# Key-value products that share a quartered stretch with attention products, output copies on ScalarE, subtractions on VectorE, loads a tile sooner

## The chip, the cores and the metric

The kernel runs on one core of one Trainium2 chip. The metric is the device time of one execution in microseconds (us). The profile's engine names are used: PE is TensorE, PEld its weight loads, DVE is VectorE, ACT is ScalarE, POOL is GpSimd, SP is SyncE, whose queue issues most DMAs. L310 is line 310 of the kernel before.

## The reference

Linear attention followed by a two-layer network with a leaky ReLU. B = 8 batches, H = 8 heads, S = 576 rows, D = 64.

```python
def _attn_ref(q, k, v):
    q_s = q - np.max(q, axis=-1, keepdims=True)
    q_s = np.exp(q_s)
    q_s = q_s / (np.sum(q_s, axis=-1, keepdims=True) + 1e-09)
    k_s = k - np.max(k, axis=2, keepdims=True)
    k_s = np.exp(k_s)
    k_s = k_s / (np.sum(k_s, axis=2, keepdims=True) + 1e-09)
    kv = np.einsum('bhsd,bhse->bhde', k_s, v)
    return np.einsum('bhsd,bhde->bhse', q_s, kv)

def _moe_ref(x, w_in, w_out):        # x: (4608, 512), w_in: (512, 2048), w_out: (2048, 512)
    h = x @ w_in
    g = np.maximum(0.01 * h, h)
    return g @ w_out
...
x = attn_out.transpose(0, 2, 1, 3).reshape(B * S, H * D)
```

Queries are normalised over the head dimension, keys over the sequence; both are needed before the small 64x64 products of a batch can be used. Almost all arithmetic is in the two layers: 4608 tokens through 512x2048 and 2048x512.

## The kernel before

**Tiling.** The 4608 tokens are cut into nine tiles t = 0 to 8 of 512 tokens. Batches have 576 tokens, so the boundaries of batches and tiles drift against each other: tile t needs the attention output of batch t - 1 or t, up to all of batch t - 1 and the first part of batch t. Layer 1 of a tile is 16 output blocks j with 4 matmuls each (L488, 128x512, weights `w_in_sb`, moving `xT`) into a PSUM tile `ph`, which ScalarE turns into `gj` with the leaky function (L497). Layer 2 is four groups `tsub` of 16 matmuls each (L509) into `pout`, which is copied to `out_sb` by `store` (L503) and written out by two DMAs on SP's queue (L506). The copy is by ScalarE for the first two groups of tile 1 and by VectorE for the rest.

**The attention part of a batch b** runs in small pieces between these matmuls:

- `load_all(b)`: three loads (k, q, v, 1152 KB each, L80), issued on SP's queue, into a pool `raw` of six buffers, so two batches' worth.
- Keys: `k_tree` (maximum over nine rows, L150) and `k_allmax` (over partitions, L155 to L175) on VectorE, `k_sub` (L183, subtract the maximum; on GpSimd for batches 3 to 7), `k_exp` on ScalarE (L191) into `ke`.
- Values: `v_cast` (L203) to bf16 on GpSimd, into one of two buffers `vb`.
- Queries: `q_max` (L214, VectorE), `q_sub` (L273, GpSimd for batches 3 to 7), `q_exp` (L281, ScalarE) into `qe`, `q_sum` (L290, L292) and `q_norm` (L297) on VectorE, and `q_turn` (L481), a DMA transpose on SP's queue into `qX`.
- `kv(b)` (L310): 72 matmuls on quarters of the array (64x64, 65 columns), four side by side, into two PSUM tiles `pkv`; then `kd_make(b)` on VectorE (L329, L330) divides by the key sums into `kd`.
- `attend_all(b, ...)` (`cross`, L429): 16 quartered matmuls with `kd` as weights and `qX` moving, eight of 512 columns (rows 0 to 7) and eight of 64 (row 8), into six PSUM tiles `po`; `x_keep` (L452) copies them into `xT` on ScalarE, four copies of 512 columns and two of 128.

**What sets the order.** The schedule is written by hand. `at(t, u, fn)` puts a piece into slot u of tile t, and `run(t, u)` emits it: slots 0 to 15 come after each block j of layer 1, slots 16 to 31 after every fourth matmul of layer 2 (slot 16 + 4 x tsub + j // 4; the output copy of a group is emitted just ahead of its last slot). A slot number of 32 or more goes on into the next tile. Each engine works through its own queue in the order of emission and waits on semaphores for its operands; a slot fixes the order within an engine, not a time. Within one slot, pieces come in the order in which they were registered.

**Slots that matter here**, for batches 3 to 7 (`plan`, L643): with t = b - 2 and an offset o of 27 (batch 3), 22 (batch 4) or 17, the tree stands at slot o of tile t, all-max and key subtraction at o + 3, query maximum and subtraction at o + 7, key exponential at o + 11, casts at o + 12, query exponential at o + 16, sum at o + 18, normalise at o + 21, transpose at o + 22, `kv` at o + 24 or o + 25. So `kv` of batch 3 falls into slot 19 of tile 2, of batch 4 into slot 15 of tile 3, of batches 5 to 7 into slot 10 of tiles 4 to 6. `attend_all` stands at slot 27 of tile b - 1 for batches 3 and 4 and at slot 23 for 5 to 7. `load_all(b)` is at slot 2 of tile b - 2. Batch 2 has a plan of its own (`plan2`, L660); the second part of its attention products stands in slot 19 of tile 2, just ahead of `kv(3)`.

**PSUM.** `psB` has six one-bank buffers, used in turn by `ph`, `po`, `pkv` and the transposes of early batches; `psO` has two for `pout`.

Of the kernel before, what the change touches and what calls it, by code (L numbers as in the profile page):

```python
# [19 lines left out]
L = 64  # L20
# [5 lines left out]
def kernel(  # L26
# [104 lines left out]
    def k_begin(b):  # L131
        st[b]["ke"] = ke_pool.tile([P, R, HL, D], BF16, name="ke")
        st[b]["kmax"] = mx_pool.tile([P, HL, D], FP32, name="kmax")
        st[b]["kmaxT"] = mx_pool.tile([P, HL * D], FP32, name="kmaxT")
        st[b]["kall"] = mx_pool.tile([P, HL, D], FP32, name="kall")

    def k_tree(b, hs, steps=slice(0, 4)):
        n = hs.stop - hs.start
        ks = st[b]["k"][:, hs]
        if steps.start == 0:  # L140
            st[b]["t4"] = mx_pool.tile([P, HL, 4, D], FP32, name="t4")[:, 0:n]
        t4 = st[b]["t4"]
        t2, t1 = t4[:, :, 0:2], t4[:, :, 0]
        for o, i0, i1 in (
            (t4, ks[:, :, 0:4], ks[:, :, 4:8]),
            (t2, t2, t4[:, :, 2:4]),
            (t1, t1, t4[:, :, 1]),
            (st[b]["kmax"][:, hs], t1, ks[:, :, 8]),
        )[steps]:
            nc.vector.tensor_tensor(out=o, in0=i0, in1=i1, op=ALU.max)  # L150

    def k_allmax(b):


        nc.vector.transpose(  # L155
            out=st[b]["kmaxT"], in_=st[b]["kmax"].rearrange("p h d -> p (h d)")
        )
        m2 = small_pool.tile([P, CB, 2], FP32, name="m2")
        nc.vector.tensor_reduce(
            out=m2[:, :, 0],  # L160
            in_=st[b]["kmaxT"].rearrange("p (c j) -> p c j", j=32),
            axis=AX.X,
            op=ALU.max,
        )
        for a in range(4):
            o = a ^ 1
            nc.vector.tensor_reduce(
                out=m2[32 * o : 32 * o + 32, :, 1],
                in_=m2[32 * a : 32 * a + 32, :, 0:1],
                axis=AX.X,  # L170
                op=ALU.max,
            )
        m = small_pool.tile([P, CB], FP32, name="m")
        nc.vector.tensor_reduce(out=m, in_=m2, axis=AX.X, op=ALU.max)
        nc.vector.transpose(  # L175
            out=st[b]["kall"].rearrange("p h d -> p (h d)"),
            in_=m.unsqueeze(2).to_broadcast([P, CB, 32]),
        )

    def k_sub(eng, b, hs):  # L180
        ks = st[b]["k"][:, hs]
        n = hs.stop - hs.start
        eng.tensor_tensor(  # L183
            out=ks,
            in0=ks,
            in1=st[b]["kall"][:, hs].unsqueeze(2).to_broadcast([P, n, R, D]),
            op=ALU.subtract,
        )

    def k_exp(b, hs):  # L190
        nc.scalar.activation(  # L191
            out=st[b]["ke"][:, :, hs].rearrange("p r h d -> p h r d"),
            in_=st[b]["k"][:, hs],
            func=AF.Exp,
        )
# [10 lines left out]
    def q_begin(b):  # L206
        st[b]["qe"] = qe_pool.tile([P, R, HL, D], BF16, name="qe")
        if b < 2:
            st[b]["qT"] = qT_pool.tile([P, NB, R, L], BF16, name="qT", tag="qT")

    def q_max(b, rs, hs=ALLH):
        n, m = rs.stop - rs.start, hs.stop - hs.start
        st[b]["qmax", rs.start, hs.start] = o = small_pool.tile([P, HL, n], FP32, name="qmax")[:, 0:m]
        nc.vector.tensor_reduce(out=o, in_=st[b]["q"][:, hs, rs], axis=AX.X, op=ALU.max)  # L214
# [55 lines left out]
    def q_sub(eng, b, rs, hs=ALLH):  # L270
        n, m = rs.stop - rs.start, hs.stop - hs.start
        qs = st[b]["q"][:, hs, rs]
        eng.tensor_tensor(  # L273
            out=qs,
            in0=qs,
            in1=st[b]["qmax", rs.start, hs.start].unsqueeze(3).to_broadcast([P, m, n, D]),
            op=ALU.subtract,
        )

    def q_exp(b, rs, hs=ALLH):  # L280
        nc.scalar.activation(  # L281
            out=st[b]["qe"][:, rs, hs].rearrange("p r h d -> p h r d"),
            in_=st[b]["q"][:, hs, rs],
            func=AF.Exp,
        )
# [160 lines left out]
    def x_keep(eng, b, ggs, rows, hp):  # L446
# [6 lines left out]
        else:  # L453
            eng.tensor_copy(out=o, in_=ps)

    def attend_rows(b, rows, engs=(nc.scalar, nc.scalar)):
        groups = ((0, 1),) if rows.stop - rows.start <= 4 else ((0,), (1,))
        for ggs in groups:
            attend(b, ggs, rows)
        return [  # L460
            lambda ggs=ggs, hp=hp: x_keep(engs[hp], b, ggs, rows, hp) for ggs in groups for hp in range(2)
        ]
# [57 lines left out]
    def at(t, u, *fns):  # L520
        while t > 0 and u >= 32:
            t, u = t + 1, u - 32
        hooks.setdefault((t, u), []).extend(fns)
# [7 lines left out]
    def load_all(b):  # L531
        whole = [(ALLH, ALLR)]
        st[b]["k"] = load(k, b, "k_raw", whole)
        st[b]["q"] = load(q, b, "q_raw", whole)
        st[b]["v"] = load(v, b, "v_raw", whole)
# [101 lines left out]
    at(1, 25, lambda: q_transpose(1, 7, 2), lambda: q_keep(nc.scalar, 1, 7, 2))  # L637

    XR = (slice(0, 6), slice(6, R))
    for b in range(3, B):  # L640
        at(b - 2, 2, lambda b=b: load_all(b))

    def plan(b, o):  # L643
        t = b - 2
        at(t, o, lambda: k_begin(b), lambda: q_begin(b), lambda: k_tree(b, ALLH))
        at(t, o + 3, lambda: k_allmax(b), lambda: k_sub(nc.gpsimd, b, ALLH))
        at(t, o + 7, lambda: q_max(b, ALLR), lambda: q_sub(nc.gpsimd, b, ALLR))
        at(t, o + 11, lambda: k_exp(b, ALLH))
        at(t, o + 12, lambda: v_cast(nc.gpsimd, b, 0), lambda: v_cast(nc.gpsimd, b, 1))
        at(t, o + 16, lambda: q_exp(b, ALLR))  # L650
        at(t, o + 18, lambda: q_sum(b, ALLR))
        at(t, o + 21, lambda: q_norm(b, ALLR))
        kvu = o + (24 if b == 3 else 25)
        at(t, kvu, lambda: kv(b))
        at(t, kvu + 1, lambda: kd_make(b))
        at(t, o + 22, lambda: q_turn(b))
        at(b - 1, 27 if b < 5 else 23, lambda: attend_all(b, (slice(0, 8),), (slice(8, R),)))


    def plan2():  # L660
        b = 2
        at(1, 0, lambda: k_tree(b, H1))
        at(1, 3, lambda: k_allmax(b))
        at(1, 6, lambda: k_sub(nc.vector, b, H0), lambda: k_sub(nc.vector, b, H1))
        at(1, 9, lambda: k_exp(b, ALLH))
        for rs in XR:
            at(1, 9, lambda rs=rs: q_max(b, rs), lambda rs=rs: q_sub(nc.gpsimd, b, rs))
        at(1, 13, lambda: v_cast(nc.gpsimd, b, 0), lambda: v_cast(nc.gpsimd, b, 1))
        for i, rs in enumerate(XR):
            at(1, (14, 16)[i], lambda rs=rs: q_exp(b, rs), lambda rs=rs: q_sum(b, rs), lambda rs=rs: q_norm(b, rs))  # L670
            at(1, (15, 17)[i], lambda rs=rs: q_turn(b, rs))
        at(1, 23, lambda: kv(b))
        at(1, 24, lambda: kd_make(b))
        at(1, 27, lambda: attend_all(b, (XR[0],)), lambda: attend_all(1, (RE,)))
        at(2, 19, lambda: attend_all(b, (XR[1],)))

    plan2()
    for b in range(3, B):
        plan(b, {3: 27, 4: 22}.get(b, 17))


    def g_tiles():
# [69 lines left out]
    for t in range(1, NT):  # L752
        g_sb = []
        for j in range(NF):
            ph = psB_pool.tile([P, TT], FP32, name="ph", tag=BANK_TAG)
            layer1(j, ph, t * TT, TT)
            if j % 2 == 0:
                g_sb.append(g_pool.tile([P, 2, TT], BF16, name="gj"))
            leaky(g_sb[j // 2][:, j % 2], ph)
            run(t, j)  # L760
        for tsub in range(NTS):
            row0 = t * TT + tsub * P
            if row0 == T - P:
                for os, copy in ((slice(0, 384), nc.scalar.copy), (slice(384, O), nc.vector.tensor_copy)):
                    po = psB_pool.tile([P, os.stop - os.start], FP32, name="pout2", tag=BANK_TAG)
                    for j in range(NF):
                        layer2(po, g_sb, tsub, j, os)
                    store(row0, po, copy, os, (nc.sync, nc.scalar))
                break
            po = psO_pool.tile([P, O], FP32, name="pout", tag="pout")  # L770
            for j in range(NF):
                layer2(po, g_sb, tsub, j)
                if j == NF - 1:
                    store(row0, po, nc.scalar.copy if t == 1 and tsub < 2 else nc.vector.tensor_copy)
                if j % 4 == 3:
                    run(t, 16 + 4 * tsub + j // 4)
    assert not hooks, list(hooks)
# [30 lines left out]
```

## Time and profile before

| What | Value |
|---|---|
| Median of 3 runs | 284.26 us (284.12 to 284.36) |
| The profiled execution | 284.65 us |
| Its span, first to last instruction | 282.9 us |
| Granted TensorE clock, mean | 0.999 |
| ScalarE, `gj` (L497), 128x512, x144 | 602 ns each |
| ScalarE, `ke` (L191), 128x2304 | 2133 ns each |
| ScalarE, `qe` (L281), 128x2304 | 2131 ns each |
| VectorE, `out_sb` copy (L503), 128x512, x33 | 687 ns each |
| VectorE, `qmax` (L214), 128x2304 | 2539 ns each |
| VectorE, `qsum` (L290) and normalise (L297), 128x2304 | 2553 and 2558 ns each |
| GpSimd, key subtraction (L183), 128x2304, x5 | 5070 ns each |
| GpSimd, query subtraction (L273), 128x2304, x5 | 4056 ns each |
| GpSimd, value cast (L203), 128x1152, x14 | 1170 ns each |
| k, q, v loads of 1152 KB, median from issue to landing | 5.9, 8.2, 10.9 us |
| `qX` transposes, issue to landing, shortest, median, longest | 3.3, 4.8, 7.0 us |

The span is counted from the first to the last instruction of the program; the profiled execution's time has some 1.75 us more around it. A matmul record's length is not its share of the engine, since matmuls overlap: the distance from one start to the next is what counts. Tiles 2 to 6 last 29.2 to 29.4 us each (layer 1 of tile 2 begins at 77.7 us, of tile 3 at 107.1, of 4 at 136.3, of 5 at 165.5, of 6 at 194.6), tiles 7 and 8 27.6 us.

### The profile page before, as it was taken

To read this page: it belongs to the slowest core of one execution; us is meant where nothing else is said; L and a number is where in the kernel's file an instruction comes from. 1 tells how busy PE (TensorE), PEld (TensorE's weight loads), DVE (VectorE), ACT (ScalarE), POOL (GpSimd) and SP (SyncE) were. 2 spreads that over 40 slices of the span, in tenths; PEclk is the share of its full clock that TensorE was granted. 3 is DMA by queue.
4 is the path that set the end of the run, shared out by engine and by line. 5 is a ranking of instruction groups with operands and counts; after the bars stand their busy time and mean duration, and the time that the engine had idled before them with its cause. 6 is when DMAs were issued, how large, how long until landed. Compare 5 with 4: busy or idle time off the path is not lost.

```text
span 282.9 us, 4998 instructions
## 1 busy us (share of the span) xinstructions
PE 275.6 (97%) x2022; PEld 133.1 (47%) x2022; DVE 143.2 (51%) x241; ACT 146.2 (52%) x258; POOL 89.6 (32%) x62
## 2 busy tenths in 40 slices
PE   8799999999999999999999999999999999999994
PEld 3367654444444544444444444444444444444443
DVE  2974889989661992596293719371801100110021
ACT  3986564693369236912963377436843165026400
POOL 2846391053078029308700780069000000000000
PEclk9999999999999999999999999999999999999999
DMA  7999999994849166953597349733053200330033
GB/s 238 333 209 326 292 173 374 318 379 162 149 126 407 41 144 151 401 99 82 132 411 107 74 92 398 170 76 74 0 86 72 59 19 0 70 81 1 0 76 74
DMA packets 37175, 45.81 MB, mean 162 GB/s; under 512 B 16032, under 2 KB 20384, under 8 KB 37152
## 3 DMA queue, kind: packets, MB, share of 16 engines
q1 hardware_dynamic: 33680, 41.16, 49.4%
q0 software_dynamic: 3312, 4.20, 8.5%
q8 instruction: 16, 0.26, 0.4%
q10 hardware_dynamic: 160, 0.13, 0.1%
q14 instruction: 7, 0.06, 0.1%
HBM read 36.70 MB, written 9.44 MB: 163 GB/s over the span
## 4 chain that ended last, share of the span: by engine, by line
PE 90%; DMA 6%; POOL 2%; SPq 0%; issue 0%; DVE 0%
PE pout L509 44%; PE ph L488 42%; DMA w_in_sb<-in_moe_w_in_dram 3%; DMA k_raw<-in_k_dram 2%; PE pkv L310 2%; PE po L429 2%; POOL w_in_sb L123 1%; POOL vb L203 0%; PE psum_q L253 0%; SPq L80 0%; POOL qe L242 0%; PE psum_qt L402 0%; DVE out_sb L503 0%; POOL gate L559 0%; POOL gate L545 0%
## 5 line engine op out<-in xcount | busy, mean ns | idle before, releaser
L509 PE MATMUL pout<-w_out_sb,gj 128*128 128x512 bf16 (+2 forms) x592 | 127.9, 373 | 0.0
L488 PE MATMUL ph<-xT,w_in_sb 128*128 128x512 bf16 (+1 forms) x640 | 127.3, 358 | 0.2 <-DMA w_in_sb<-in_moe_w_in_dram 0.2
L497 ACT ACTIVATE gj<-ph 128x512 bf16<-128x512 f32 x144 | 81.8, 602 | 53.8 <-PE ph L488 53.4
L488 PEld LDWEIGHTS <-w_in_sb 128*128 128x128 bf16 x640 | 62.0, 98 | 62.1 <-DMA w_in_sb<-in_moe_w_in_dram 0.9
L509 PEld LDWEIGHTS <-gj 128*128 128x128 bf16 x592 | 56.4, 98 | 64.7 <-issue 0.2
L503 DVE COPY out_sb<-pout 128x512 f32<-128x512 f32 (+1 forms) x34 | 22.7, 675 | 89.9 <-PE pout L509 87.1
L183 POOL TENSOR_TENSOR k_raw<-k_raw,kall 128x2304 f32<-128x2304 f32 (+1 forms) x6 | 29.1, 4857 | 75.6 <-DVE kall L175 62.1
L452 ACT CAST xT<-po 128x512 bf16<-128x512 f32 (+3 forms) x43 | 17.0, 488 | 43.4 <-PE po L429 43.4
L273 POOL TENSOR_TENSOR q_raw<-q_raw,qmax 128x2304 f32<-128x2304 f32 (+4 forms) x12 | 32.3, 2694 | 22.1 <-DVE qmax L214 21.4
L290 DVE TENSOR_REDUCE qsum<-qe 128x36 f32<-128x2304 bf16 (+5 forms) x13 | 20.1, 1543 | 30.7 <-ACT qe L281 30.7
L297 DVE TENSOR_TENSOR qe<-qe,qrec 128x2304 bf16<-128x2304 bf16 (+5 forms) x13 | 22.3, 1717 | 0.4
L191 ACT ACTIVATE ke<-k_raw 128x2304 bf16<-128x2304 f32 (+2 forms) x11 | 17.6, 1603 | 6.6 <-POOL k_raw L183 5.4
L214 DVE TENSOR_REDUCE qmax<-q_raw 128x36 f32<-128x2304 f32 (+5 forms) x13 | 19.9, 1537 | 0.8 <-DMA q_raw<-in_q_dram 0.8
L281 ACT ACTIVATE qe<-q_raw 128x2304 bf16<-128x2304 f32 (+5 forms) x13 | 17.2, 1325 | 2.9 <-POOL q_raw L273 2.9
L203 POOL CAST vb<-v_raw 128x1152 bf16<-128x1152 f32 x14 | 16.0, 1170 | 0.0
L150 DVE TENSOR_TENSOR t<-k_raw 128x512 f32<-128x512 f32 (+1 forms) x11 | 10.2, 927 | 2.7 <-DMA k_raw<-in_k_dram 2.7
L150 DVE TENSOR_TENSOR t<-t 128x256 f32<-128x256 f32 (+2 forms) x22 | 9.9, 449 | 0.7
L503 ACT COPY out_sb<-pout 128x512 f32<-128x512 f32 (+1 forms) x3 | 1.7, 550 | 15.7 <-PE pout L509 15.7
L341 PE MATMUL pout<-zero 128*128 128x512 bf16 x24 | 8.3, 488 | 1.3 <-POOL zero L98 1.3
L310 PEld LDWEIGHTS <-ke 64*64 64x64 bf16 x576 | 5.8, 106 | 3.3 <-ACT gj L497 1.7
L310 PE MATMUL pkv<-vb,ke 64*64 64x65 bf16 x576 | 6.9, 194 | 0.2
L228 ACT ACTIVATE qe<-q_raw,nmax 128x64 bf16<-128x64 f32 x16 | 5.3, 333 | 3.5 <-DVE nmax L223 3.5
(59 smaller groups left out, 90.2 us busy)
## 6 DMA issues: line engine op xcount, KB each, us to landing
out_dram<-out_sb SPq DMA_DIRECT2D x70, 128.0 KB, 2.4
v_raw<-in_v_dram SPq DMA_DIRECT2D x7, 1152.0 KB, 10.9
q_raw<-in_q_dram SPq DMA_DIRECT2D x6, 1152.0 KB, 8.2
k_raw<-in_k_dram SPq DMA_DIRECT2D x5, 1152.0 KB, 5.9
k_raw<-in_k_dram SPq DMA_DIRECT2D x6, 576.0 KB, 6.2
w_in_sb<-in_moe_w_in_dram POOLq DMA_DIRECT2D x8, 256.0 KB, 7.7
w_out_sb<-in_moe_w_out_dram POOLq DMA_DIRECT2D x6, 256.0 KB, 11.4
v_raw<-in_v_dram SPq DMA_DIRECT2D x2, 576.0 KB, 7.5
```

What stands on the lines that cost most here:

```text
L150: nc.vector.tensor_tensor(out=o, in0=i0, in1=i1, op=ALU.max)
L183: eng.tensor_tensor(out=ks, in0=ks, in1=st[b]["kall"][:, hs].unsqueeze(2).to_broadcast([P, n, R, D]), op=ALU.subtract,)
L191: nc.scalar.activation(out=st[b]["ke"][:, :, hs].rearrange("p r h d -> p h r d"), in_=st[b]["k"][:, hs], func=AF.Exp,)
L214: nc.vector.tensor_reduce(out=o, in_=st[b]["q"][:, hs, rs], axis=AX.X, op=ALU.max)
L273: eng.tensor_tensor(out=qs, in0=qs, in1=st[b]["qmax", rs.start, hs.start].unsqueeze(3).to_broadcast([P, m, n, D]), op=ALU.subtract,)
L290: nc.vector.reduce_sum(out=qsum, in_=st[b]["qe"][:, rs, hs], axis=AX.X)
L297: nc.vector.tensor_tensor(out=qes, in0=qes, in1=st[b]["qrec", rs.start, hs.start].unsqueeze(3).to_broadcast([P, n, m, D]), op=ALU.mult,)
L310: nc.tensor.matmul(outs[hh][hp * D : (hp + 1) * D, 0 : D + 1], lhsT=st[b]["ke"][rows, r, 2 * gg + hp], rhs=vb2[b % 2][rows, r, gg, hp, 0 : ...
L488: nc.tensor.matmul(ph, lhsT=w_in_sb[:, cb, j * P : (j + 1) * P], rhs=xT[:, cb, c0 : c0 + n], start=(cb == 0 and first), stop=(cb == NB - 1 ...
L497: nc.scalar.activation(out=o, in_=ph, func=AF.Prelu, alpha=LEAKY_SLOPE)
L503: copy(out=out_sb, in_=pout)
L509: nc.tensor.matmul(pout, lhsT=g_sb[j // 2][:, j % 2, tsub * P : (tsub + 1) * P], rhs=w_out_sb[:, j, os], start=(j == 0), stop=(j == NF - 1),)
```

## The change

- **A new function `attend_kv(b)`** takes the place of `attend_all(b)` for batches 3 to 6. It emits the attention products of batch b for rows 0 to 7 as before, then takes two PSUM tiles that each hold row 8's attention products (128 columns) and, behind them, the key-value sums of batch b + 1 (2 x 66 columns); it emits row 8's products into the first part and then the 72 key-value matmuls of batch b + 1 into the second. `kd_make(b + 1)` follows on VectorE, and the six `x_keep` copies on ScalarE. So the key-value products of batches 4 to 7 no longer have slots of their own. Batch 3's stay at slot 19 of tile 2, and batch 7's attention keeps `attend_all`.
- **Subtractions** of keys and queries of batches 3 to 7 go from GpSimd to VectorE.
- **Output copies** of tiles 1 to 7 are all on ScalarE; tiles 0 and 8 are unchanged.
- **Loads**: batch 4's go from slot 2 of tile 2 to slot 17 of tile 1 (behind batch 2's second transpose on SP's queue), batch 5's from slot 2 of tile 3 to slot 9 of tile 2, batches 6 and 7 from slot 2 of tiles 4 and 5 to slot 5 of tiles 3 and 4 (behind the transpose of the batch before the last loaded).
- **The slots of the softmax steps** are set anew (`k_front`, `q_front`, `casts`, `q_back`), mostly earlier, since a batch's keys are wanted sooner.

```diff
+    def attend_kv(b, rows=slice(0, 8), rest=slice(8, R)):
+        keep = attend_rows(b, rows)
+        n = 2 * (rest.stop - rest.start) * L
+        both = [psB_pool.tile([P, n + 2 * (D + 2)], FP32, name="pokv", tag=BANK_TAG) for _ in range(2)]
+        ps = [a[:, 0:n].rearrange("p (g c) -> p g c", g=2) for a in both]
+        st[b + 1]["pkv"] = pkv = [a[:, n:].rearrange("p (g d) -> p g d", g=2) for a in both]
+        for gg in range(2):
+            cross(b, gg, [ps[hp][:, gg] for hp in range(2)], rest)
+        for gg in range(2):
+            kv_quads(b + 1, gg, [pkv[hh][:, gg] for hh in range(2)])
+        st[b]["po", (0, 1), rest.start] = ps
+        kd_make(b + 1)
+        for fn in keep:
+            fn()
+        for hp in range(2):
+            x_keep(nc.scalar, b, (0, 1), rest, hp)
...
-    for b in range(3, B):
-        at(b - 2, 2, lambda b=b: load_all(b))
-
-    def plan(b, o):
-        t = b - 2
...
-        at(b - 1, 27 if b < 5 else 23, lambda: attend_all(b, (slice(0, 8),), (slice(8, R),)))
+    at(1, 2, lambda: load_all(3))
...
+        at(1, 17, lambda: load_all(4))
         at(1, 23, lambda: kv(b))
         at(1, 24, lambda: kd_make(b))
         at(1, 27, lambda: attend_all(b, (XR[0],)), lambda: attend_all(1, (RE,)))
         at(2, 19, lambda: attend_all(b, (XR[1],)))
...
+    def k_front(b, t, u, v):
+        at(t, u, lambda: k_begin(b), lambda: q_begin(b), lambda: k_tree(b, ALLH))
+        at(t, v, lambda: k_allmax(b), lambda: k_sub(nc.vector, b, ALLH))
+
+    def q_front(b, t, u):
+        at(t, u, lambda: q_max(b, ALLR), lambda: q_sub(nc.vector, b, ALLR))
+
+    def casts(b, t, u):
+        at(t, u, lambda: v_cast(nc.gpsimd, b, 0), lambda: v_cast(nc.gpsimd, b, 1))
+
+    def q_back(b, t, u):
+        at(t, u, lambda: q_sum(b, ALLR), lambda: q_norm(b, ALLR), lambda: q_turn(b))
+
+    k_front(3, 1, 25, 25)
+    q_front(3, 1, 28)
+    casts(3, 2, 0)
+    at(2, 2, lambda: k_exp(3, ALLH))
+    k_front(4, 2, 7, 17)
+    at(2, 8, lambda: q_exp(3, ALLR))
+    q_back(3, 2, 9)
+    at(2, 9, lambda: load_all(5))
+    casts(4, 2, 12)
+    at(2, 19, lambda: kv(3), lambda: kd_make(3))
+    at(2, 22, lambda: k_exp(4, ALLH))
+    at(2, 27, lambda: attend_kv(3))
+    for t in range(3, B - 1):
+        b = t + 1
+        q_front(b, t - 1, 29)
+        at(t, 2, lambda b=b: q_exp(b, ALLR))
+        if b + 1 < B:
+            k_front(b + 1, t, 1, 8)
+            casts(b + 1, t, 6)
+            at(t, 17, lambda b=b: k_exp(b + 1, ALLH))
+            at(t, 23, lambda b=b: attend_kv(b))
+        else:
+            at(t, 23, lambda b=b: attend_all(b, (slice(0, 8),), (slice(8, R),)))
+        q_back(b, t, 5)
+        if b + 2 < B:
+            at(t, 5, lambda b=b: load_all(b + 2))
...
-                    store(row0, po, nc.scalar.copy if t == 1 and tsub < 2 else nc.vector.tensor_copy)
+                    store(row0, po, nc.scalar.copy if t < NT - 1 else nc.vector.tensor_copy)
```

## The prediction

> **What bounds the kernel now.** I read the page first (busy shares, then the chain that ended last), then that chain in order of time, then TensorE's timeline around every stretch that is not a plain run of 128x512 matmuls.
>
> ```profile
> span 282.9 us, 4998 instructions
> PE 275.6 (97%) x2022; PEld 133.1 (47%) x2022; DVE 143.2 (51%) x241; ACT 146.2 (52%) x258; POOL 89.6 (32%) x62
> PE 90%; DMA 6%; POOL 2%; SPq 0%; issue 0%; DVE 0%
> ```
>
> ```profile
> 107.09 13.81 PE ph L488 x64
> 120.91 0.73 PE pkv L310 x72
> 121.64 10.47 PE pout L509 x48
> ```
>
> The second fence is the chain in order of time (start, us, what). One tile of 512 tokens is 64 layer-1 and 64 layer-2 matmuls at 13.81/64 = 0.216 us from start to start, and beside them only the small stretches: key-value products (L310) and attention products (L429). From 48 us to the end nothing but TensorE is on the chain, and TensorE's own list of waits holds nothing after that time. So time goes only if TensorE is given less to do, and comes only if TensorE is made to wait. What a small stretch costs is read off the timeline (start, us, line; the stretch begins at the last full matmul before it):
>
> ```profile
> 119.66 1.24 PE L488 MATMUL ph<-xT,w_in_sb 128*128 128x512 bf16 x5
> 120.83 0.80 PE L310 MATMUL pkv<-vb,ke 64*64 64x65 bf16 x72
> 121.57 0.82 PE L509 MATMUL pout<-w_out_sb,gj 128*128 128x512 bf16 x3
> ...
> 131.08 1.03 PE L509 MATMUL pout<-w_out_sb,gj 128*128 128x512 bf16 x4
> 132.03 0.69 PE L429 MATMUL po<-qX,kd 64*64 64x512 bf16 x16
> 132.65 1.25 PE L509 MATMUL pout<-w_out_sb,gj 128*128 128x512 bf16 x5
> ...
> 93.71 1.24 PE L509 MATMUL pout<-w_out_sb,gj 128*128 128x512 bf16 x5
> 94.88 0.36 PE L429 MATMUL po<-qX,kd 64*64 64x192 bf16 x8
> 95.07 0.83 PE L310 MATMUL pkv<-vb,ke 64*64 64x65 bf16 x72
> 95.83 0.82 PE L509 MATMUL pout<-w_out_sb,gj 128*128 128x512 bf16 x3
> ...
> 173.51 1.46 PE L488 MATMUL ph<-xT,w_in_sb 128*128 128x512 bf16 x6
> 174.90 0.78 PE L310 MATMUL pkv<-vb,ke 64*64 64x65 bf16 x72
> 175.61 0.82 PE L488 MATMUL ph<-xT,w_in_sb 128*128 128x512 bf16 x3
> ```
>
> The last full matmul before batch 4's key-value products starts at 119.66 + 4 x 0.216 = 120.52, the next full one at 121.57: 1.05 us, of which 0.216 is the slot that it would have had anyway, so the stretch costs 0.83. Batch 5's (145.40 to 146.44) is the same; batch 6's (174.59 to 175.61) and 7's take 1.02, cost 0.80. An attention stretch runs 131.73 to 132.65, 0.92 to 0.93, cost 0.71. Each has an entry (last full start to first quarter start) of 0.30 to 0.31, against 0.216 between full ones, and an exit: the last 64-column group starts about 0.5 us into the attention stretch and the first full matmul follows 0.13 later, where the next group of four would have followed after 0.03. The third group of lines is the one place where both kinds already share a stretch (attention of batch 2, key-value of batch 3): 94.57 to 95.83, 1.26 us, and the key-value part begins 0.19 after the attention part, as soon as two groups of 192 columns are through (about 0.09 each). No entry and no exit are paid between them.
>
> **The change, part by part.**
>
> *Shared stretches.* Batches 4 to 7 lose their own stretch; their 72 matmuls follow the 16 of the batch before. Batch 3 already shares one. New length: entry 0.31, attention part 0.51 (0.69 less the 0.19 of its last matmul, plus one step), key-value part 0.74 (alone, 120.83 to 121.57) to 0.76 (behind attention, 95.07 to 95.83): 1.56 to 1.58, cost 1.34 to 1.36. Before: 0.83 + 0.71 = 1.54 for batches 4 and 5, 0.80 + 0.71 = 1.51 for 6 and 7. Saved: 0.18 to 0.20 twice and 0.15 to 0.17 twice, together 0.66 to 0.74. The first full matmul after each exit also comes 0.01 late (0.226 for 0.216), saved four times. I take **0.7 us**, bounds 0.6 and 0.8. The number of matmuls is unchanged.
>
> *Output copies to ScalarE* (four per tile, 0.59 each by its own rows, against 0.69 on VectorE). They cost nothing on the path while ScalarE keeps up. Per tile of 29.2 us it gets 16 x 0.60 (activations) + 2 x 2.13 (exponentials) + 2.4 (attention copies) + 4 x 0.59 = 18.6. The tight places are where a copy goes ahead of attention copies that the next tile needs. Batch 3: copy about 103.15 to 103.75, six attention copies (2.39, L452) to 106.15, while TensorE first runs 16 full matmuls and the added key-value part and wants them near 107.6: 1.4 us spare. Tile 1 to 2: 73.6 + 0.59 + 2.18 = 76.4 against 77.52: 1.1 spare. Without that cover each microsecond late is one on the path.
>
> ```profile
> L183 DVE TENSOR_TENSOR k_raw<-k_raw,kall 128x1152 f32<-128x1152 f32 x3 | 4.0, 1355 | 0.1
> L503 ACT COPY out_sb<-pout 128x512 f32<-128x512 f32 x2 | 1.2, 586 | 3.4 <-PE pout L509 3.4
> ```
>
> *Subtractions to VectorE.* A whole one (2304 columns) has no VectorE row. Bounds: two of the 1152 rows, 2.71, and 2.53 (the qmax reduction of the same 2304 columns); I take 2.6, against POOL's 5.07 (keys) and 4.06 (queries). VectorE gains 5.2 per tile and loses 4 x 0.69. It is off the path, and copies that waited for TensorE no longer stand in its queue.
>
> *Is the chain ready for the earlier products?* They are due 17 us sooner (batch 4: 120.8 becomes 103.4). Following VectorE's queue: free at 71.0, keys of 3 (tree and all-max 5.2 as at 74.21 to 79.37, subtraction 2.6), queries of 3 (2.53 + 2.6) to 83.9; tree of 4 (2.85) to 86.8. ScalarE does batch 3's query exponential behind activation 8 (86.2 to 88.3), then VectorE has qsum 2.55, reciprocal 0.38, normalise 2.56, all-max 2.3, subtraction 2.6 = 10.4, with issue steps 10.6: 98.9. Key exponential to 101.1, needed at about 103.4: **2.3 us spare**. In tile 3 the same reckoning gives queries of 4 ready at 110.5 (wanted 111.0), keys of 5 exponentiated by 126.0, due 128.8: 2.8 spare; in tiles 4 and 5 about 3. kd_make waits for TensorE in VectorE's queue, as before, and what stands behind it (q_front) has 4 us from tile 4 on.
>
> *Loads and transposes on SP.* Batch 4's three loads (0.5 each to issue) now stand behind the second qX transpose (issue ends 72.4) and ahead of three tiles' output stores, which go 1.7 later; out_sb has four buffers and the next copy is 20 us off. Keys landed 5.9, values 10.9 after issue: about 79 and 85, wanted at 83.9 and before 103. Batch 5's load waits behind batch 3's transpose, which waits for normalise (94.0): issue 96, keys at 102, wanted 110.5. Transposes land 3.3 to 7.0 after issue, so qX of 3 by 101.0, wanted 102.8. Raw buffers are free (key exponential of 3 at 83, query at 88). Value casts stay on POOL, now alone there: nothing.
>
> **A rule against it.** The new tile keeps the eighth row's attention products and the key-value sums in one PSUM bank; at 95.07 they had separate banks, so no row covers this. The Trainium skill (TensorEngine Tiling (Array Packing), Gotcha 1: PSUM Pressure) says that different row tiles cannot access one bank at the same time. Here row half 0 writes the first bank and half 1 the second in both kinds of product, so by that rule nothing changes.
>
> **The rivals.**
> 1. *The shared bank serialises* (half the gain). If the key-value part waits until the last attention group has drained, the 0.13 less 0.03 of an exit comes back four times: saving 0.7 - 0.4 = 0.3, 283.95. For: untried in the trace. Against: the halves keep to their banks.
> 2. *Slower: the VectorE chain of 10.6 us from query exponential to key subtraction comes late for L310 in tiles 3 to 5.* POOL's casts may collide with VectorE's two-input operations; for it, the row below, 3.79 where half of 5.07 is 2.54, with VectorE subtracting beside it. (The Trainium skill, SBUF — State Buffer, Who interferes with whom, states the same contention.) It decides once the chain is over 13.4 (27% longer). At 40% TensorE waits 1.4 at three stretches: +4.2 - 0.7, 287.8; at 32%, 0.6 each, 285.4. Against: casts run when their values land, beside operations that have slack, save the query subtraction of 4, and even 1.2 there leaves 1.6.
>
> ```profile
> L183 POOL TENSOR_TENSOR k_raw<-k_raw,kall 128x1152 f32<-128x1152 f32 x1 | 3.8, 3790 | 0.5 <-DVE kall L175 0.5
> ```
>
> 3. *The merge gives nothing, or small waits eat it* (an attention copy 0.2 late at a tile's start, a matmul issued late behind more semaphores): 284.2 to 284.4.
>
> **How the numbers follow.** The profiled execution took 284.65, span 282.9, so 1.75 lies around it. The span becomes 282.2, that execution 283.95; the median shown is 0.39 under it, so **283.55**. Chances: this 0.68, rival 1 0.10, rival 2 0.12, rival 3 0.10. Own range of the first: 283.4 to 283.75. Reaching to rivals 1 and 3 gives 283.3 to 284.4 (0.86, less tails). About 0.2% (0.57 us) is what a measurement tells from no change, and the forecast of 0.25% is only just over it: of the first case I count 0.6 as faster and 0.08 as same; rival 1 and most of 3 are same. Faster 0.61, same 0.25, slower 0.14.
>
> **What would show it.** Right: four stretches of 16 + 72 quarter matmuls, 1.56 to 1.58 from full start to full start, no L310 stretch alone after 70 us, no TensorE wait after 48 us. Wrong: those stretches near 1.7 (rival 1); L310 or L488 waiting for ke or xT, tile 3 worst (rival 2); key subtractions on VectorE well over 2.7.

## The result, and the profile after

The changed kernel takes 283.61 us (median of 20 runs, 283.44 to 284.61) against 284.36 us before (20 runs beside them): ratio 0.9975, 95% interval 0.9966 to 0.9984. The forecast was 283.55 us, 0.25% less. A second set of runs of the same kernel (e9 below) gave 0.9978 (0.9968 to 0.9988).

The page of the changed kernel (profiled execution 284.27 us), its span and its busy shares:

```profile
span 282.5 us, 4982 instructions
PE 273.0 (97%) x1995; PEld 133.4 (47%) x2022; DVE 159.0 (56%) x225; ACT 160.9 (57%) x284; POOL 53.3 (19%) x52
```

VectorE and ScalarE are each 15 us busier and GpSimd 36 us less, and none of that is on the path: TensorE's list of waits after 48 us names no other engine, as before. The span says little by itself, since tile 1 began 0.2 us later in this execution (48.37 against 48.16 us, the first layer-1 record of that tile), before anything that the change touches. Counted from there to the end, 234.72 us became 234.13: 0.59 us less. This stretch is used below, because it repeats well (234.13 and 234.16 in two profiles of the changed kernel).

TensorE's timeline around the first and the last shared stretch (start, us, line, operation, tiles, shapes, count):

```profile
101.67 1.46 PE L526 MATMUL pout<-w_out_sb,gj 128*128 128x512 bf16 x6
103.05 0.63 PE L429 MATMUL po<-qX,kd 64*64 64x512 bf16 x8
103.51 0.23 PE L429 MATMUL pokv<-qX,kd 64*64 64x64 bf16 x8
103.57 0.87 PE L310 MATMUL pokv<-vb,ke 64*64 64x65 bf16 x72
104.37 0.82 PE L526 MATMUL pout<-w_out_sb,gj 128*128 128x512 bf16 x2
...
185.54 1.24 PE L526 MATMUL pout<-w_out_sb,gj 128*128 128x512 bf16 x5
186.71 0.63 PE L429 MATMUL po<-qX,kd 64*64 64x512 bf16 x8
187.17 0.23 PE L429 MATMUL pokv<-qX,kd 64*64 64x64 bf16 x8
187.23 0.81 PE L310 MATMUL pokv<-vb,ke 64*64 64x65 bf16 x72
187.97 0.39 PE L526 MATMUL pout<-w_out_sb,gj 128*128 128x512 bf16 x1
```

Read as before: the last full matmul starts at 101.67 + 5 x 0.216 = 102.75, the next at 104.37, so 1.62 us from full to full; the last stretch runs 186.40 to 187.97, 1.57. (After 104.37 and after 187.97 the profile lacks a record: "x2" in 0.82 us, "x1" in 0.39.) The four measure 1.624, 1.624, 1.599 and 1.573, 6.42 in all; e9's profile, which lacks no record, has the same four within 0.001. Before, the four lone key-value stretches (1.045, 1.045, 1.020, 1.019) and the four attention stretches (0.928, 0.928, 0.929, 0.929) were 7.84 together. Four full-matmul slots of 0.216 less are contained in the new ones, so 7.84 - 6.42 - 4 x 0.216 = 0.56, and with the 0.01 saved at each of four exits 0.60: the whole gain of 0.59 that the profile shows.

### The profile page after: what moved, and what is told of

The parts are those of the page before. It is cut to its first block, busy times and chain, and to the rows that moved or that the text cites. A ratio compares the mean times of both kernels' runs of the same rounds, so it can differ in the third digit from the quotient of the medians.

```text
span 282.5 us, 4982 instructions
## 1 busy us (share of the span) xinstructions
PE 273.0 (97%) x1995; PEld 133.4 (47%) x2022; DVE 159.0 (56%) x225; ACT 160.9 (57%) x284; POOL 53.3 (19%) x52
## 4 chain that ended last, share of the span: by engine, by line
PE 84%; DMA 10%; POOL 3%; issue 1%; SPq 0%; ACT 0%; DVE 0%; ACTq 0%; POOLq 0%
PE pout L526 42%; PE ph L505 39%; DMA w_out_sb<-in_moe_w_out_dram 5%; DMA w_in_sb<-in_moe_w_in_dram 3%; DMA k_raw<-in_k_dram 2%; PE po L429 2%; POOL w_in_sb L123 1%; PE pokv L310 1%; POOL w_out_sb L128 1%; PE pkv L310 1%; POOL vb L203 0%; SPq L80 0%; POOL qe L242 0%; PE psum_q L253 0%; ACT gj L514 0%
## 5 line engine op out<-in xcount | busy, mean ns | idle before, releaser
L526 PE MATMUL pout<-w_out_sb,gj 128*128 128x512 bf16 (+2 forms) x575 | 126.6, 373 | 2.0 <-DMA w_out_sb<-in_moe_w_out_dram 0.9
L520 ACT COPY out_sb<-pout 128x512 f32<-128x512 f32 (+1 forms) x29 | 16.8, 580 | 66.7 <-PE pout L526 43.0
L520 DVE COPY out_sb<-pout 128x512 f32<-128x512 f32 (+1 forms) x8 | 4.8, 637 | 70.8 <-PE pout L526 70.8
L203 POOL CAST vb<-v_raw 128x1152 bf16<-128x1152 f32 x14 | 24.7, 1793 | 81.7 <-DMA v_raw<-in_v_dram 60.1
L183 DVE TENSOR_TENSOR k_raw<-k_raw,kall 128x2304 f32<-128x2304 f32 (+1 forms) x8 | 16.8, 2107 | 0.3
L452 ACT CAST xT<-po 128x512 bf16<-128x512 f32 (+3 forms) x35 | 15.7, 537 | 1.6 <-PE po L429 1.6
L273 POOL TENSOR_TENSOR q_raw<-q_raw,qmax 128x512 f32<-128x512 f32 (+3 forms) x7 | 12.0, 1720 | 22.8 <-DVE qmax L214 22.1
L150 DVE TENSOR_TENSOR t<-t 128x256 f32<-128x256 f32 (+2 forms) x22 | 14.8, 674 | 0.7
L150 DVE TENSOR_TENSOR t<-k_raw 128x512 f32<-128x512 f32 (+1 forms) x11 | 12.1, 1102 | 2.4 <-DMA k_raw<-in_k_dram 2.2
L273 DVE TENSOR_TENSOR q_raw<-q_raw,qmax 128x2304 f32<-128x2304 f32 (+1 forms) x6 | 13.2, 2203 | 0.3
```

What stands on the lines that cost most here:

```text
L203: eng.tensor_copy(out=o, in_=i)
L273: eng.tensor_tensor(out=qs, in0=qs, in1=st[b]["qmax", rs.start, hs.start].unsqueeze(3).to_broadcast([P, m, n, D]), op=ALU.subtract,)
L520: copy(out=out_sb, in_=pout)
L526: nc.tensor.matmul(pout, lhsT=g_sb[j // 2][:, j % 2, tsub * P : (tsub + 1) * P], rhs=w_out_sb[:, j, os], start=(j == 0), stop=(j == NF - 1),)
```

## The experiments

Each starts from the changed kernel. The comparisons are with the kernel before, on the same chip.

### e1: the stretches apart again

```diff
-    at(2, 27, lambda: attend_kv(3))
+    at(2, 26, lambda: kv(4), lambda: kd_make(4))
+    at(2, 27, lambda: attend_all(3, (slice(0, 8),), (slice(8, R),)))
...
-            at(t, 23, lambda b=b: attend_kv(b))
+            at(t, 22, lambda b=b: kv(b + 1), lambda b=b: kd_make(b + 1))
+            at(t, 23, lambda b=b: attend_all(b, (slice(0, 8),), (slice(8, R),)))
```

> Theory (the gain is four mode changes of TensorE fewer, nothing else): with the key-value products of batches 4 to 7 back in stretches of their own, one slot ahead of the attention products, and everything else as changed, four lone L310 stretches of about 1.03 us and four attention stretches of 0.93 us come back, where the changed kernel has four shared ones of 1.57 to 1.62. The time from tile 1's first layer-1 matmul to the end goes from 234.0 back to about 234.6 us, the whole to about 284.2, ratio to before 0.999 to 1.001. Rival (the relief of VectorE and GpSimd, or the earlier loads, gave the time): it stays at about 283.6, ratio 0.9975.

Measured: 284.28 us (12 runs), ratio 1.0003 (0.9993 to 1.0012); from tile 1 to the end 234.77. TensorE's timeline in tile 3:

```profile
126.54 1.46 PE L526 MATMUL pout<-w_out_sb,gj 128*128 128x512 bf16 x6
127.93 0.80 PE L310 MATMUL pkv<-vb,ke 64*64 64x65 bf16 x72
128.67 1.04 PE L526 MATMUL pout<-w_out_sb,gj 128*128 128x512 bf16 x4
129.63 0.69 PE L429 MATMUL po<-qX,kd 64*64 64x512 bf16 x16
130.25 0.61 PE L526 MATMUL pout<-w_out_sb,gj 128*128 128x512 bf16 x2
```

Four full matmuls stand between the two kinds again, and the whole gain is gone, though copies, subtractions and loads stay as changed. So these parts give no time; the shared stretch gives all of it.

### e2: both subtractions back on GpSimd

```diff
-        at(t, v, lambda: k_allmax(b), lambda: k_sub(nc.vector, b, ALLH))
+        at(t, v, lambda: k_allmax(b), lambda: k_sub(nc.gpsimd, b, ALLH))
...
-        at(t, u, lambda: q_max(b, ALLR), lambda: q_sub(nc.vector, b, ALLR))
+        at(t, u, lambda: q_max(b, ALLR), lambda: q_sub(nc.gpsimd, b, ALLR))
```

> Changed kernel with the subtractions of batches 3 to 7 back on GpSimd. Theory (VectorE's subtraction is what makes the earlier key-value products possible): the key subtraction of batch 4 ends about 101.7 instead of 99.2, its exponential about 103.8, 0.2 to 0.5 us after TensorE wants it; in tile 3 the query subtraction (4.06 for 2.56) and the key subtraction (5.07 for 2.56) together make it 0.5 to 1.5 late; tiles 4 and 5 just hold. In all 0.7 to 2 us more than the changed kernel: 284.3 to 285.6. Rival (the subtractions are hidden on either engine, the spare 2.3 us was enough): 283.6, no wait at the shared stretches.

Measured: 287.19 us (5 runs), ratio 1.0091 (1.0076 to 1.0105), 3.6 over the changed kernel by the medians: the mechanism as expected, the size too small. TensorE's timeline in tile 3, then a line of VectorE's and one of GpSimd's a little earlier, and the key subtraction of the changed kernel for comparison:

```profile
129.23 0.63 PE L429 MATMUL po<-qX,kd 64*64 64x512 bf16 x8
129.68 0.23 PE L429 MATMUL pokv<-qX,kd 64*64 64x64 bf16 x8
131.64 0.80 PE L310 MATMUL pokv<-vb,ke 64*64 64x65 bf16 x72 [1.72 <-ACT ke L191]
```

```profile
109.60 5.70 DVE L150 TENSOR_TENSOR t<-t 128x512 f32<-128x512 f32 x2
124.39 5.04 POOL L183 TENSOR_TENSOR k_raw<-k_raw,kall 128x2304 f32<-128x2304 f32 x1 [8.07 <-DVE kall L175]
```

```profile
122.78 2.56 DVE L183 TENSOR_TENSOR k_raw<-k_raw,kall 128x2304 f32<-128x2304 f32 x1
```

The key-value part of tile 3 waits 1.72 us for the key exponential (tile 2's stretch grew from 1.62 to 2.44, that of tile 3 to 3.45). Beside GpSimd's query subtraction and casts, two steps of VectorE's maximum tree took 5.70 us, where the kernel before needed 1.15; the expectation had no such term. But e8 below has the same 5.70 us and no wait: most of the lateness is the key subtraction's, 5.04 us on GpSimd for 2.56 on VectorE. A second cost was not foreseen at all. The windows of the same run (us; busy time of PE, PEld, DVE, ACT, POOL; granted TensorE clock; DMA share; GB/s):

```profile
132.30:134.00 1.70, 1.70 (x19) 0.72 (x10) 1.44 (x5) 1.70 (x5) 0.00 (x0) 0.59 1.04 412
134.00:136.00 2.00, 2.00 (x7) 0.63 (x6) 2.00 (x2) 0.83 (x4) 0.01 (x1) 0.50 1.05 406
136.00:138.00 2.00, 2.00 (x11) 0.94 (x10) 1.97 (x2) 0.23 (x1) 2.00 (x1) 0.99 0.28 101
```

Right after the wait the granted clock falls to 0.50 for some 3.4 us, and full matmuls come 0.427 us apart, not 0.216: about eight of them, some 1.7 us on top of the wait. The profiled execution is the slowest of the five (288.62 us, 4.7 more than the changed kernel from tile 1 to the end: 3.0 of longer small stretches and this 1.7). Its mean clock is 0.993; three of the other four, the median among them, have 1.000, so the 3.6 us stand without this second cost.

### e3: output copies back on VectorE

```diff
-                    store(row0, po, nc.scalar.copy if t < NT - 1 else nc.vector.tensor_copy)
+                    store(row0, po, nc.scalar.copy if t == 1 and tsub < 2 else nc.vector.tensor_copy)
```

> Changed kernel with the output copies of tiles 1 (last two) to 7 back on VectorE. Theory (copies are off the path on either engine): query steps stand behind a copy that waits for TensorE and start up to 1 us later, within the 2.3 to 3 us spare; shared stretches unchanged, 283.5 to 283.8. Rival (ScalarE copies are needed, since VectorE's queue is then held by TensorE's pace): the key exponentials come late in tiles 3 to 5, 0.5 us or more at each, 285 or more.

Measured: 285.09 us (7 runs), ratio 1.0031 (1.0019 to 1.0043). The theory missed, and the rival had the amount but not the place: the shared stretches stayed at 1.624 to 1.572, and TensorE waited once, in tile 2. VectorE's timeline and then TensorE's:

```profile
96.75 2.56 DVE L183 TENSOR_TENSOR k_raw<-k_raw,kall 128x2304 f32<-128x2304 f32 x1
99.23 0.68 DVE L520 COPY out_sb<-pout 128x512 f32<-128x512 f32 x1
```

```profile
95.34 3.63 PE L526 MATMUL pout<-w_out_sb,gj 128*128 128x512 bf16 x16
99.96 1.24 PE L526 MATMUL pout<-w_out_sb,gj 128*128 128x512 bf16 x5 [1.00 <-DVE out_sb L520]
```

Tile 2's first `pout` was finished by about 94.5 us, but its copy stood behind the key subtraction of batch 4 until 99.23. `pout` has two PSUM buffers; the third group of layer 2 needs the first one back, and its first matmul starts 1.16 us late (98.59 to 99.96 instead of 0.216 on). From tile 1 to the end: 235.28, 1.15 over the changed kernel (1.5 by the medians).

### e7: the same, with tile 2's copies on ScalarE

```diff
+                    store(row0, po, nc.scalar.copy if t == 2 or t == 1 and tsub < 2 else nc.vector.tensor_copy)
```

> Output copies on VectorE again as in e3, but those of tile 2 on ScalarE. Theory (e3 lost its time at one place: tile 2's first copy stood behind the key subtraction of batch 4 on VectorE, and the third layer-2 group waited for its PSUM buffer): no wait of TensorE is left, the time is that of the changed kernel, 283.5 to 283.7. Rival (copies on VectorE delay the later tiles too): 284 to 285.

Measured: 283.74 us (11 runs), ratio 0.9978 (0.9969 to 0.9988), 234.17 from tile 1 to the end, no wait. One tile's copies decide, the other twenty-odd are free on either engine.

### e4: the loads at their old slots

```diff
-        at(1, 17, lambda: load_all(4))
...
-    at(2, 9, lambda: load_all(5))
+    at(2, 2, lambda: load_all(4))
+    at(3, 2, lambda: load_all(5))
...
-            k_front(b + 1, t, 1, 8)
+            k_front(b + 1, t, 3, 8)
...
-            at(t, 5, lambda b=b: load_all(b + 2))
+            at(t + 1, 2, lambda b=b: load_all(b + 2))
```

> Changed kernel with the loads of batches 4 to 7 at their old slots (slot 2 of tile b - 2; the tree of the batch behind them at slot 3). Theory: batch 5's keys land about 6 us after an issue near 111 us, VectorE's queue stands still at the tree until 117 with the normalising of batch 4 behind it, and the key exponential comes 3 to 4 us after TensorE wants it in each of tiles 3, 4 and 5: 8 to 13 us more, 292 to 297. Rival (the loads had enough lead already): about 283.6.

Measured: 292.0 us (one run, so without an interval). VectorE's timeline in tile 3:

```profile
107.32 2.56 DVE L273 TENSOR_TENSOR q_raw<-q_raw,qmax 128x2304 f32<-128x2304 f32 x1
115.94 1.23 DVE L150 TENSOR_TENSOR t<-k_raw 128x1024 f32<-128x1024 f32 x1 [6.06 <-DMA k_raw<-in_k_dram]
```

VectorE stands still 6.06 us for the keys, with the normalising of batch 4 behind the tree in its queue, and the shared stretches of tiles 3, 4 and 5 grow to 4.39, 3.70 and 3.49 us: 2.8, 2.1 and 1.9 more, each less than the 3 to 4 expected. In the first, 0.38 us of it is a wait for the transpose into `qX`. After the first the clock was again at half for a while (0.58 on average over 132 to 136 us); after the two others it was not. The longer stretches make 6.8 of the 8.3 us that this profile has more from tile 1 to the end, and the half clock most of the rest.

### e8: query subtractions alone on GpSimd

```diff
-        at(t, u, lambda: q_max(b, ALLR), lambda: q_sub(nc.vector, b, ALLR))
+        at(t, u, lambda: q_max(b, ALLR), lambda: q_sub(nc.gpsimd, b, ALLR))
```

> Changed kernel with the query subtractions alone back on GpSimd (key subtractions stay on VectorE). Theory (e2 lost its time through the key subtraction, which stands right before the exponential that TensorE waits for; the query subtraction has slack in tile 2 and uses up the 1.7 us that tile 3 has): 283.6 to 284.0, at most 0.3 of waiting at tile 3's shared stretch. Rival (both count alike): half of e2's loss, 285 or more.

Measured: 284.02 us (10 runs), ratio 0.9992 (0.9981 to 1.0003), at the upper edge of what was expected; its profile has 234.39 from tile 1 to the end, 0.26 over the changed kernel: 0.13 more at tile 3's stretch (1.75) and 0.13 at slot 19 of tile 2. Neither is a wait. The key exponential of batch 5 and its use in tile 3:

```profile
125.84 2.12 ACT L191 ACTIVATE ke<-k_raw 128x2304 bf16<-128x2304 f32 x1 [3.83 <-DVE k_raw L183]
128.72 1.00 PE L310 MATMUL pokv<-vb,ke 64*64 64x65 bf16 x72
```

The exponential ends at 127.96, 0.76 us before its use; the changed kernel has 1.7 us there. So the query subtraction takes 0.9 us of spare time and no time of TensorE's, and most of e2's lateness belongs to the key subtraction. What TensorE lost here is one pause of 0.11 to 0.12 us in the middle of the 72 key-value starts, in each of the two stretches. Such pauses (0.08 to 0.12) also stand in three stretches of e2 that wait for nothing, and a smaller one (0.06) in tile 2 of e7, whose subtractions are as changed. What makes them is not shown, so whether the query subtraction costs this 0.26 stays open.

### e5, e6: the order inside the shared stretch

In the changed kernel the key-value part took 0.62 to 0.66 us from first to last start; alone it had been 0.58 to 0.59. By the single records, matmuls start in fours 29 to 36 ns apart at first, and later one by one, some 8 ns apart with pauses of 16 to 34 ns between. Two orders test why. The diff is e5's; e6 has one loop instead, in which `attend(b, (gg,), rows)` follows `kv_quads` of the same half:

```diff
-        for gg in range(2):
-            cross(b, gg, [ps[hp][:, gg] for hp in range(2)], rest)
         for gg in range(2):
             kv_quads(b + 1, gg, [pkv[hh][:, gg] for hh in range(2)])
+        for gg in range(2):
+            attend(b, (gg,), rows)
+        for gg in range(2):
+            cross(b, gg, [ps[hp][:, gg] for hp in range(2)], rest)
```

> Changed kernel with the order inside the shared stretches turned round: 72 key-value matmuls, then the 512-column attention groups, then row 8. Theory (the key-value part took 0.62 to 0.66 us from first to last start, against 0.58 to 0.59 alone, because TensorE's instructions arrive at about 8.3 ns each and what had queued up during the full matmuls before is used up by the attention products first): the key-value part falls back to 0.58 to 0.59, the stretches from 1.57 to 1.62 to about 1.53 to 1.55; 0.2 to 0.3 us less, 283.3 to 283.4. Rival (the shared bank or the change of operands costs the 0.06, whatever the order): stretches stay at 1.57 to 1.62.

> Changed kernel with the two 512-column attention groups set between the key-value matmuls (36, group, 36, group, row 8). Theory (instructions queue up while a 512-column group streams): both halves of the key-value part run at the pace of the array, about 30 ns for four, 0.27 each; stretches 1.45 to 1.52, 0.4 to 0.5 us less than the changed kernel, 283.1 to 283.3, ratio to before 0.996. Rival (the pace is that of the array or the weight loads, not of the queue): 1.57 to 1.62 as before.

TensorE's timeline of e5 in tile 3:

```profile
126.86 1.46 PE L530 MATMUL pout<-w_out_sb,gj 128*128 128x512 bf16 x6
128.24 0.80 PE L310 MATMUL pokv<-vb,ke 64*64 64x65 bf16 x72
128.86 0.62 PE L429 MATMUL po<-qX,kd 64*64 64x512 bf16 x8
129.30 0.25 PE L429 MATMUL pokv<-qX,kd 64*64 64x64 bf16 x8
129.47 0.61 PE L530 MATMUL pout<-w_out_sb,gj 128*128 128x512 bf16 x2
```

e5: 283.35 us (5 runs), ratio 0.9962 (0.9949 to 0.9976). From 126.86 + 5 x 0.216 = 127.94 to 129.47 are 1.54 us; the four stretches are 1.607, 1.541, 1.517, 1.515, of which one lies in the 1.53 to 1.55 expected, two just under it and tile 2's far over it; the key-value part took 0.58 to 0.59 in all four, as expected, and the four stretches together 0.24 less. e6: 283.51 us (6 runs), ratio 0.9969 (0.9957 to 0.9980), stretches 1.618, 1.556, 1.556, 1.556: better than the changed kernel by 0.13, but not the 1.45 to 1.52 that was expected. By the single records its halves of 36 took 0.29 and 0.30 us (0.32 in tile 2): behind a 512-column group the second half again starts in fours, at the pace of a stretch alone. What was too low is the 0.27 expected for a half. The order matters, which speaks against the rival that the bank or the operands cost the 0.06. That an empty instruction queue is the cause fits e5 and e6, but it was argued from the order and not shown by itself. Tile 2's stretch gains least in both, mostly because of one pause of 0.07 to 0.09 us ahead of an attention group, 0.01 to 0.03 in the other tiles; its cause stays open.

### e9, e10: the changed kernel beside the better order

e10 is e5, with batch 3's key-value matmuls ahead of batch 2's attention products at slot 19 of tile 2 as well; e9 is the changed kernel again.

```diff
-        at(2, 19, lambda: attend_all(b, (XR[1],)))
...
-    at(2, 19, lambda: kv(3), lambda: kd_make(3))
+    at(2, 19, lambda: kv(3), lambda: kd_make(3), lambda: attend_all(2, (XR[1],)))
```

> The changed kernel once more, beside the next run on one chip. All theories: 283.5 to 283.7, ratio to before about 0.9975, the four shared stretches at 1.57 to 1.63 us.

> As e5 (key-value matmuls first in the shared stretches), and batch 3's key-value matmuls ahead of batch 2's attention products too. Theory (the pace depends on how many instructions have queued up): the four stretches at 1.52 to 1.61 as in e5, batch 3's from 1.27 to about 1.24; 0.25 to 0.3 us under the changed kernel, 283.3, ratio to before about 0.996. Rival (e5's 0.26 in the median was chance): the same time as the changed kernel beside it, within 0.1.

e9: 283.50 us (12 runs), ratio 0.9978 (0.9968 to 0.9988). e10: 283.36 us (12 runs), ratio 0.9971 (0.9961 to 0.9982). In the profiles e10 has 233.82 us from tile 1 to the end against 234.16: 0.34 less (e5: 233.88), with batch 3's stretch at 1.21 instead of 1.27 and the others as in e5. The times go the same way, but 0.14 us between two medians with overlapping intervals doesn't establish it; the profiles, two of each order, show it for TensorE's own part.

## Why the prediction was right

- **What bounds the kernel.** Right: TensorE without a wait before and after, and the time moved by what TensorE was spared. e1 shows that nothing else of the change gave any.
- **The shared stretches.** The mechanism was right (one entry and one exit less, four times). The term was a little too large: 0.7 us forecast, 0.60 by the stretches, 0.59 from tile 1 to the end. The medians differ by 0.75 (0.45 to 0.97 by the interval of the ratio), so that 283.61 came out so near 283.55 is partly luck. What was mis-sized is the key-value part behind attention: set at 0.74 to 0.76 by two rows, it took 0.80, 0.80, 0.77 and 0.75 (103.57 to 104.37 in the first), in tiles 2 to 5. It depends on what stands ahead of it: with the order turned round (e5) it is back at 0.58 to 0.59 from first to last start, and the stretches fall by 0.24 in all. Batch 3's row of before, from which the 0.76 came, stood behind two short groups of 192 columns, not behind 512-column ones.
- **Is the chain ready.** Tile 2: key exponential forecast to end at 101.1 and wanted at 103.4; it ended at 101.34 and its use began at 103.57, 2.2 us spare for the 2.3 forecast. Tile 3: forecast 126.0 with 2.8 spare, measured 127.50 with 1.7; tiles 4 and 5: 3.4 each for "about 3". Tile 3's shortfall is rival 2's mechanism, without its result. VectorE's timeline of the changed kernel and GpSimd's, then the same steps before:

```profile
110.42 2.17 DVE L150 TENSOR_TENSOR t<-k_raw 128x1024 f32<-128x1024 f32 x1
112.61 1.98 DVE L150 TENSOR_TENSOR t<-t 128x512 f32<-128x512 f32 x2
```

```profile
109.76 3.82 POOL L203 CAST vb<-v_raw 128x1152 bf16<-128x1152 f32 x2 [21.56 <-PE ph L505]
```

```profile
88.52 2.25 POOL L203 CAST vb<-v_raw 128x1152 bf16<-128x1152 f32 x2
98.09 1.21 DVE L150 TENSOR_TENSOR t<-k_raw 128x1024 f32<-128x1024 f32 x1
99.34 1.15 DVE L150 TENSOR_TENSOR t<-t 128x512 f32<-128x512 f32 x2
```

  The casts of batch 5 ran beside the tree, not only beside the query subtraction as forecast: two took 3.82 us for 2.25 before, and the tree's steps 2.17 and 1.98 for 1.21 and 1.15. (The Trainium skill, SBUF — State Buffer, Who interferes with whom, has VectorE's two-input operations contend with GpSimd's reads; these rows agree.) It cost a microsecond of spare time and none on the path.
- **Subtractions.** 2.6 forecast, 2.56 measured. That the shared stretch depends on them was said as spare time only; e2 prices both at 3.6 us, and by e8 most of it is the key subtraction.
- **Copies.** "Nothing while ScalarE keeps up" held. The prediction did not see that they had to move: with the subtraction on VectorE, tile 2's copies there cost 1.2 by the profile, 1.5 by the medians (e3).
- **Loads.** Forecast as enough; in e4's one run the old slots cost 8 us.
- **Rivals.** 1 (shared bank): no gap between the two kinds, the first key-value group follows 0.06 after row 8's first (103.51, 103.57), which leaves no room for a drain. 2 and 3: no wait appeared.

## What to carry to other kernels

When one engine is dense, count how often it changes between full and small products: grouping the small ones saved 0.15 us a time, while 36 us taken off GpSimd gave nothing by themselves. Moving work earlier has enablers that look like gains and aren't; price each by putting it back alone (here 1.5, 3.6 and 8 us by the run times, the last from one run). Where two engines' queues meet in a buffer of two, ask what stands ahead of the copy that frees it, not how busy the copying engine is.

## What the hardware showed that was not expected

- A wait of TensorE of 1.72 us (e2) and one of 2.16 (e4) were each followed by a granted clock of 0.50 for some 3.4 us, with full matmuls 0.427 us apart; e4's two later waits, of 1.99 and 1.79 us, were not, and e2's mean clocks (0.993 in the profiled execution, 1.000 in three of the other four) show that it doesn't come in every execution. The Trainium skill (TensorE: Matmul & The Clock Gate, Part 1: The HAM clock gate) puts the return to half rate at an idle window of about 3.4 us; here shorter waits were enough, and not every time. With the small products around the wait, it was 3.45 us (e2) and 4.39 us (e4) from the start of the last full matmul to that of the next, but also 3.70 and 3.49 us in the two cases without effect.
- The pace of 72 small quartered matmuls depends on what runs before them: 0.58 to 0.59 us from first to last start behind full matmuls (0.61 once, in e1), 0.62 to 0.66 behind attention products. Only behind attention products was there also a pause of 0.06 to 0.12 us among them, in some stretches of e2, e7 and e8 (0.72 to 0.79 in all).
